# An adaLN block on one NeuronCore: early feed-forward weights, sums in DRAM, block modulation, two-bank ScalarE reads and a new warm-up tile

## The chip, the cores and the metric

One of the eight cores of a Trainium2 chip runs the whole program. The metric is the device time of one execution in microseconds; lower is better. Five engines have their own instruction streams: TensorE (PE, with its weight loads PEld), VectorE (DVE), ScalarE (ACT), GpSimd (POOL) and SyncE (SP), whose queue issues nearly all DMAs.

## The reference

The input x has 2048 tokens of 512 features, in fp32. Six modulation rows come from one product of a 512-vector with a 512 x 3072 matrix.

```python
mod = (silu(c) @ w_mod).reshape(c.shape[0], 6, 1, -1)
sa, ca, ga, sb, cb, gb = (mod[:, i] for i in range(6))
h = layernorm(x) * (1 + ca) + sa
x = x + ga * A(h)          # 32 heads of 16, 4 segments of 512 tokens
h = layernorm(x) * (1 + cb) + sb
x = x + gb * (relu(h @ w1 + b1) ** 2 @ w2 + b2)     # 512 -> 1792 -> 512
```

A projects h to q, k and v. In each segment it does causal softmax attention, reads a memory matrix M (16 x 16 a head) with phi(q) = where(q > 0, q + 1, exp(q)), mixes the two by a gate per head, and after the segment adds phi(k)^T v to M. The result goes through wo.

## The kernel before

Every fp32 operand of a large product is split into a rounded high part and the rest; a product is then three matmuls (high x high, high x low, low x high).

**Start.** Four token tiles of segment 0 and the 512 x 512 blocks of w_mod for sa and ca are loaded (`load_x`, `mod_cols`). TensorE runs warm-up products on `msk`, a tile that POOL clears (L438, L439, L546). `mod_parts` multiplies silu(c) with whole rows (L568), ScalarE copies the result (L572), and four small products a vector turn it into columns `modc` (L588, L590). Tiles are normalized (L607), turned (L616), scaled and shifted (L628, L630) and split into `HT` (L636, L638). The first q and k products (`qk` of unit 0, L747 to L749) follow.

**Attention.** There are 16 units (4 segments x 4 groups of eight heads). For each, `qk` projects (L757), ScalarE and VectorE split (L794, L796), and twelve DMAs spread the parts over the rows of `ST`, a ring of 12 slots (L812). `vproj` makes v once a segment (L837), and eight ScalarE copies put it into `VT` (L829). `a_quad` computes scores for the row maxima (L870), VectorE reduces them (L875), except the tile `ac` that ScalarE copies (L908) for POOL and VectorE; the maxima are turned (L940), negated (L942) and sent into `ST`. `b_quad` computes scores again with the maximum taken off; a pair of products fills two PSUM banks, and ScalarE takes exp of each bank (L1057); POOL masks (L1044); the products with v follow (L1099). `mem` reads and updates M (L967, L991, L993, L1001).

**Output projection and feed-forward.** `wo_tile` turns the attention result (L1241), splits it (L1248, L1250), multiplies (L1214 to L1216) and adds x (L1257). The last segment's four tiles come at the end, because they need unit 15 (L1161 to L1170). `ln2` makes seven combinations of the normalized tokens. The first layer is one step of a Strassen scheme over 2 x 2 blocks: seven products (`prod`, L1443 to L1445) in place of eight, for each of seven column pairs q and four segments. `load_w1` loads a pair (L1390), splits three blocks (L1396 on ScalarE, L1399 on VectorE), forms four sums in place (L1404, four VectorE operations) and splits these. It does so for each of the 28 pairs. `ffn1` adds up the products and squares; `ffn2` multiplies with W2 (L1502 to L1504).

**Order.** Every step is a node made by `op`, with an engine, a planned duration and the nodes it waits for. `ORDER` holds, for each engine, the node numbers in the order in which they are emitted; an engine runs them in that order. `Plan.take` gives a product its PSUM bank, the first free one. The tiles of the feed-forward stage lie in a pool that is opened when every node of the attention stage has been emitted (`open_ffn`, N_FFN).

Of the kernel before, what the change touches and what calls it, by code (L numbers as in the profile page):

```python
# [8 lines left out]
F32 = mybir.dt.float32  # L9
F32R = mybir.dt.float32r  # L10
# [8 lines left out]
P = 128  # L19
# [15 lines left out]
N_WARM = 70  # L35
# [28 lines left out]
395 520 320 280 405 324-325 434 439 392 326 407 437 446 328 449 397 330 413 442 539 768 528 769 454 770 549 771 533
547 773-774 558 775-776 552 530 421 458-460 423 415 525 462 469 873 472 429 465 935 535 936 644 477 937 657 938 431
481 561 482-483 652 563 940 570 941 573 682 942 544 943 801-802 654 566 803-804 578 649 806-807 554 808 485 809 663
487 582-583 586 668 589 584 685 671 593 659 601 596 673 1345-1346 1355-1356 676 605-607 687 835 1006 1068 694 1069 678
1070 702 848 609 1071 611 854 1073 690 1074 845 1075 697 843 1076 876 706 840 710 707-708 717 818 867 819-820 850 821
725 720 864 823-824 713 859 825 862 826 968 729 976 882 730-731 889 981 1201 869 1202 973 987 1203 978 1204 897 995
1206 1139 892 1207 885 1208 983 1209 1101 1109 879 901-902 905 733 912 903 735 915 908 992 920 1009 1000 997 924-925  # L70
1015 1106 926 1012 1018 1114 1022 1025 1002 928 1111 1142 930 1030 1034 1145 1120 1133 1038 1035-1036 1128 1045 1041
1272 1048 1363 1053 1364 1116 1365 1125 1234 1366 1242 1057-1059 1130 1148 1368 1155 1369 1151 1370 1135 1371 1163
1061 1253 1063 1167 1247 1396-1397 1239 1398-1399 1158 1266 1401-1402 1171 1403 1244 1404 1258 1168-1169 1178 1530
1181 1261 1531 1174 1532-1533 1263 1275 1186 1535-1536 1249 1537 1430 1438 1538 1468 1190-1192 1281 1413 1288 1414
1284 1415 1194 1416 1296 1196 1291 1418-1419 1268 1420 1449 1459 1443 1421 1278 1940-1941 1950-1951 1457 1435
1300-1302 1440 1304 1601 1311 1663 1314 1664 1454 1307 1665 1445 1666 1563 1471 1462 1668-1669 1319 1670 1464 1576
1671 1571 1474 1323 1582 1324-1325 1573 1796 1477 1797 1484 1798 1568 1492 1799 1487 1592 1801 1578 1802 1604 1590
1480 1803 1327 1804 1696 1329 1496 1595 1500 1497-1498 1607 1587 1507 1503 1734 1706 1510 1515 1519 1709 1610 1613
1520-1521 1617 1704 1597 1523 1620 1525 1737 1701 1625 1629 1740 1715 1633 1723 1630-1631 1640 1636 1958 1711 1959
1829 1842 1960 1834 1961 1867 1643 1963-1964 1648 1837 1965 1870 1966 1720 1652-1654 1873 1839 1743 1656 2114 1750  # L80
# [1479 lines left out]
```

## Time and profile before

| | |
|---|---|
| Median of 3 runs | 774.13 us (774.03 to 775.08) |
| Profiled execution, whole | 778.38 us |
| Its span, first to last instruction | 776.7 us |
| Mean granted TensorE clock | 0.993 |
| Busy in the span | PE 756.3, DVE 643.3, ACT 509.2, POOL 233.6 us |

The profile is of one execution. A matmul's row gives its start and a modelled end; neighbouring matmuls overlap, so the time from one start to the next is what a product costs. A row of the timeline has start, length, engine, line, operation, out<-in, shape and count, and in brackets the idle time before it with what ended it. "PE ... <- ACT ..." in the view of waits says that TensorE waited for ScalarE. PEclk is the share of the full TensorE clock that was granted in a stretch.

### The profile page before, as it was taken

How to read it: one execution, taken by the hardware profiler on the slowest of the kernel's cores; microseconds unless marked ns; L12 is line 12 of the kernel's file. 1: busy time of each engine (PE TensorE's matmuls, PEld its weight loads, DVE VectorE, ACT ScalarE, POOL GpSimd, SP SyncE). 2: the span in 40 equal slices, each digit the busy share in tenths (PEclk: the TensorE clock that was granted, in tenths of full speed). 3: DMA queues.
4: the chain of work that ended last, by engine and by line, in shares of the span. 5: the costliest groups of instructions: out<-in, count | busy, mean ns of one | idle time of the engine just before them, and what ended most of it. 6: DMA issues, size and time to landing. Idle time of an engine off the chain costs nothing.

```text
span 776.7 us, 17899 instructions
## 1 busy us (share of the span) xinstructions
PE 756.3 (97%) x6576; PEld 594.2 (77%) x6579; DVE 643.3 (83%) x1643; ACT 509.2 (66%) x990; POOL 233.6 (30%) x351
## 2 busy tenths in 40 slices
PE   8998999999999999999999989999999999999998
PEld 4777657675787858875676668888888888998896
DVE  3577877897888897789889889999989998998753
ACT  0658768879779896778756836667555665655541
POOL 3555453537665786534513310000000010000000
PEclk9999999999999999999999999999999999999999
DMA  7574661330443324244654166322351121043201
GB/s 270 174 182 107 203 182 52 89 98 23 118 124 83 98 71 103 55 116 127 167 176 132 49 201 192 96 82 82 108 174 58 41 96 55 28 136 101 63 1 54
DMA packets 78097, 84.81 MB, mean 109 GB/s; under 512 B 9014, under 2 KB 47674, under 8 KB 78011
## 3 DMA queue, kind: packets, MB, share of 16 engines
q1 hardware_dynamic: 77858, 83.55, 37.4%
q8 instruction: 52, 0.85, 0.5%
q14 instruction: 35, 0.28, 0.1%
q10 hardware_dynamic: 152, 0.13, 0.1%
HBM read 46.16 MB, written 10.49 MB: 73 GB/s over the span
## 4 chain that ended last, share of the span: by engine, by line
PE 69%; DVE 16%; ACT 6%; issue 3%; SPq 3%; DMA 2%; POOL 1%; ACTq 0%; DVEq 0%; POOLq 0%
PE bqk L757 9%; PE bpv L1099 6%; PE bpf L1502 5%; PE bpf L1504 5%; PE bpf L1503 5%; PE ba L870 5%; PE bpb L1040 5%; PE bv L837 4%; PE bhy L1443 3%; PE bhy L1444 2%; PE bhy L1445 2%; ACT pt L1057 2%; SPq L812 2%; PE bwarm L546 2%; DVE w1r L1404 2%
## 5 line engine op out<-in xcount | busy, mean ns | idle before, releaser
L875 DVE CUSTOM_DVE_ANT_0 ba<-ba,msk 128x128 f32<-128x128 f32 (+2 forms) x384 | 186.0, 542 | 33.9 <-PE ba L870 27.1
L1057 ACT ACTIVATE pt<-bpb 128x512 f32<-128x512 f32 x320 | 173.3, 616 | 31.2 <-PE bpb L1040 27.6
L1044 POOL TENSOR_SCALAR_AFFINE_SELECT pt<-pt 128x512 f32<-128x512 f32 x128 | 80.6, 649 | 93.4 <-ACT pt L1057 63.3
L1396 ACT CAST w1d<-w1r 128x768 fp32r<-128x768 f32 (+1 forms) x56 | 52.7, 944 | 76.5 <-PE bhy L1445 58.2
L757 PE MATMUL bqk<-HT,WQK 64*128 64x512 f32 x720 | 101.6, 396 | 0.0
L1502 PE MATMUL bpf<-W,rr 128*128 128x512 f32 x224 | 88.7, 396 | 0.0
L1504 PE MATMUL bpf<-W,rr 128*128 128x512 f32 x224 | 88.0, 393 | 0.0
L1503 PE MATMUL bpf<-W,rr 128*128 128x512 f32 x224 | 87.7, 391 | 0.0
L1099 PE MATMUL bpv<-pt,VT 128*32 128x512 f32 (+3 forms) x1024 | 81.3, 442 | 0.9 <-DVE mx L875 0.4
L1040 PE MATMUL bpb<-ST 64*128 64x256 f32 (+2 forms) x512 | 79.4, 350 | 2.3 <-ACT phi L803 0.4
L870 PE MATMUL ba<-ST 63*128 63x256 f32 (+2 forms) x512 | 75.1, 346 | 1.0 <-issue 0.4
L757 PEld LDWEIGHTS bqk<-HT,WQK 64*128 64x128 f32 x720 | 69.7, 186 | 8.2 <-issue 0.6
L1040 PEld LDWEIGHTS bpb<-ST 64*128 64x128 f32 x512 | 50.0, 185 | 21.2 <-ACT pt L1057 3.9
L870 PEld LDWEIGHTS ba<-ST 63*128 63x128 f32 x512 | 48.8, 187 | 19.4 <-issue 4.2
L1399 DVE TENSOR_TENSOR w1d<-w1r,w1d 128x768 fp32r<-128x768 f32 (+1 forms) x56 | 60.6, 1085 | 3.2 <-ACT w1d L1396 2.8
L1099 PEld LDWEIGHTS bpv<-pt,VT 128*32 128x32 f32 x1024 | 27.7, 110 | 38.1 <-issue 29.5
L837 PE MATMUL bv<-WVO,HT 64*128 64x512 f32 x384 | 54.9, 405 | 0.0
L875 DVE DVE_READ_ACCUMULATOR2_ANT mx<- 128x1 f32 x384 | 54.1, 141 | 0.0
L603 POOL TENSOR_SCALAR st_all<-st_all 128x4 f32<-128x4 f32 x4 | 1.8, 451 | 169.8 <-DVE st_all L596 169.8
L1404 DVE TENSOR_TENSOR w1r<-w1r 128x256 f32<-128x256 f32 x112 | 47.5, 424 | 3.2
L1481 ACT ACTIVATE r<-r,b1c 128x512 f32<-128x512 f32 x56 | 38.4, 719 | 17.8 <-DVE r L1463 17.5
L1504 PEld LDWEIGHTS bpf<-W,rr 128*128 128x128 f32 x224 | 42.0, 188 | 10.0 <-DVE rr L1489 0.3
(200 smaller groups left out, 1829.6 us busy)
## 6 DMA issues: line engine op xcount, KB each, us to landing
ST<-sg SPq DMA_DIRECT2D x192, 128.0 KB
w1r<-in_B_w SPq DMA_DIRECT2D x56, 256.0 KB
wm<-in_w_mod SPq DMA_DIRECT2D x24, 256.0 KB
xt<-in_A_x SPq DMA_DIRECT2D x16, 256.0 KB
xw<-in_A_x SPq DMA_DIRECT2D x16, 256.0 KB
wr<-in_B_w SPq DMA_DIRECT2D x14, 256.0 KB
o_dram<-on SPq DMA_DIRECT2D x12, 256.0 KB
ot<-o_dram SPq DMA_DIRECT2D x12, 256.0 KB
```

The costliest lines, as they stand in the source:

```text
L757: m = nc.tensor.matmul(bank(("qk", u, w)), W3(w, k, x, cc * P, (cc + 1) * P)[z], HT[z, y, k], start=(ph == 0 and k == 0 and i == 0), stop= ...
L837: m = nc.tensor.matmul(bank(("v", s, t)), HT[z, x, k, t * P:(t + 1) * P], WVO[z, k, y], start=(ph == 0 and k == 0 and i == 0), stop=(ph == ...
L870: nc.tensor.matmul(dst[:, c0:c0 + n], ST[b:b + 63, 0, sl, qt * P:(qt + 1) * P], ST[b:b + 63, 1, sl, :n], start=True, stop=True)
L875: nc.vector.tensor_tensor_reduce(i, i, msk[:, 512 - n:], scale=1.0, scalar=-3e38, op0=ALU.add, op1=ALU.max, accum_out=o)
L1040: nc.tensor.matmul(dst, ST[b:b + 64, 1, sl, kb * P:(kb + 1) * P], ST[b:b + 64, 0, sl, q0:512], start=True, stop=True)
L1044: nc.gpsimd.affine_select(out=ap, in_=ap, pattern=[[0, ap.shape[1]], [1, P]], compare_op=ALU.is_ge, fill=0.0, base=0, channel_multiplier=-1)
L1057: ns = [act(512, lambda j=j: nc.scalar.activation(buf("PPP"[n], pt)[:, i + j], bank(keys[j]), AF.Exp, scale=0.25), pr[slot] + 0.01 + 0.001 ...
L1099: nc.tensor.matmul(bank(o)[32 * hq:32 * hq + 32, q0:q0 + src.shape[1]], v[:, a:a + 32], src, start=start, stop=stop, tile_position=(0, 32 ...
L1404: nc.vector.tensor_tensor(r[:, o], r[:, a], r[:, b], op=f)
L1502: nc.tensor.matmul(p, rh, FF["W2"][:, f, 0], start=(f == 0), stop=False)
L1503: nc.tensor.matmul(p, rh, FF["W2"][:, f, 1], start=False, stop=False)
L1504: nc.tensor.matmul(p, rl, FF["W2"][:, f, 0], start=False, stop=(f == NF - 1))
```

## The change

1. **Warm-up.** 46 products in place of 70; they read a 128 x 128 tile `wz` that VectorE clears first, read four times over.
2. **Block modulation.** sa and ca are computed in four blocks of 128 features: two loads of 512 x 128 (rows of 512 bytes) a block, eight products with the block as weights and 64 equal columns, and one VectorE addition into `modc`. The whole-row products, the two ScalarE copies and the turning products of these two vectors go. The affine step of a feature block waits for its own block only, and the first q and k products for the first half of `HT`.
3. **ScalarE over neighbouring banks.** All of PSUM is one tile `PB`. `banks` gives a pair of products two banks side by side where it can, and one ScalarE instruction then reads both: exp, `ac`, `mt`, `pk` and the copies into `VT`. Where they are not side by side, two are issued.
4. **Early feed-forward weights.** `ST`, `SG` (the split q and k) and `AC` live to the end. Raw pairs of w1 go into `SG`, their split forms and the results `rr` into slots of `ST`; pairs 0 and 1 no longer wait for N_FFN but for the last users of these places. `u` uses the `xr` tiles.
5. **Sums in DRAM.** The first segment stores each pair's four sums (one DMA of 512 KB a pair); the other three load them instead of forming them (21 loads more, 7 stores more, 84 VectorE operations fewer) and load three of the four raw blocks.
6. **Order.** All five lists are new, with other constants in the planner. Numbers are not comparable between the lists, since nodes were added and removed.

```diff
-N_WARM = 70
+N_WARM = 46
...
+    def banks(self, k):
+        free = set(self.pools["bank"])
+        near = lambda i: (i - 1 in free) + (i + 1 in free)
+        if k == 2:
+            pairs = [(i, i + 1) for i in sorted(free) if i + 1 in free]
...
+    wz = const.tile([P, P], BF, name="wz")
+    nc.vector.memset(wz, 0.0)
...
-    ST = sb.tile([P, 2, NSLOT, 512], F32R, name="ST")
+    ST = const.tile([P, 2, NSLOT, 512], F32R, name="ST")
+    SG = const.tile([P, 4, 512], F32R, name="SG")
+    AC = const.tile([P, 2, 512], F32, name="AC")
...
+    PB = ps.tile([P, 8, 512], F32, name="PB")
...
+    def both(keys, f):
+        a, b = (PL.slot[k] for k in keys)
+        if b == a + 1:
+            f(PB[:, a:b + 1], slice(0, 2))
+        else:
+            f(PB[:, a:a + 1], slice(0, 1))
+            f(PB[:, b:b + 1], slice(1, 2))
...
-        pe("F", 0.22, lambda: nc.tensor.matmul(bank(wk_), msk[:, :P], msk, start=True, stop=True), 50.0,
+        pe("F", 0.22, lambda: nc.tensor.matmul(bank(wk_).rearrange("p (a n) -> p a n", a=4), wz, wz[:, None, :].to_broadcast([P, 4, P]), start=True, stop=True), 50.0,
...
-    n_ca = mod_cols(1, CA, 1.0, PR0 + 0.1, pool="P")
-    n_sa = mod_cols(0, SA, 0.0, PR0 + 0.2, pool="P")
-    MODC = {CA: [n_ca, n_sa]}
+    NR = 64
+    def mod_block(j):
+        c = slice(j * P, (j + 1) * P)
+        ld = [sp(lambda m=m: nc.sync.dma_start(buf("P", keys_m[m])[:, :, c],
+                                               wmod[:, m * D + j * P:m * D + (j + 1) * P].rearrange("(k p) n -> p k n", p=P)),
...
+        def mm():
+            for m in (0, 1):
+                for k in range(KD):
+                    nc.tensor.matmul(bank(b_m)[:, NR * (2 * j + m):NR * (2 * j + m + 1)], TL[keys_m[m]][:, k, c],
+                                     cs[:, k:k + 1].to_broadcast([P, NR]), start=k == 0, stop=k == KD - 1)
...
+    MODC = {CA: [mod_block(j) for j in range(KD)]}
...
-                           after=[n] if k else [*ht, *(WN[w, cc] if s == 0 else []), *ends], get=() if k or i else [("#D", b)])
+                           after=[n, *(ht[2:] if k == 2 else [])] if k else [*ht[:2], *(WN[w, cc] if s == 0 else []), *ends], get=() if k or i else [("#D", b)])
...
-        cp = [act(512, lambda j=j: nc.scalar.copy(buf("ac", ac)[:, j], bank(keys[j])), pr[0] + 0.01 + 0.001 * j, after=[first],
-                  put=[keys[j]]) for j in (0, 1)]
+        cp = [act(1024, lambda: both(keys, lambda p, w: nc.scalar.copy(buf("ac", ac)[:, w], p)), pr[0] + 0.01, after=[first], put=keys)]
...
-            ns = [act(512, lambda j=j: nc.scalar.activation(buf("PPP"[n], pt)[:, i + j], bank(keys[j]), AF.Exp, scale=0.25),
-                      pr[slot] + 0.01 + 0.001 * j, after=[k], put=[keys[j]]) for j in (0, 1)]
+            ns = [act(1024, lambda: both(keys, lambda p, w: nc.scalar.activation(buf("PPP"[n], pt)[:, i + w.start:i + w.stop], p, AF.Exp, scale=0.25)),
+                      pr[slot] + 0.01, after=[k], put=keys)]
...
+        first = s == 0 and q < 2
+        ks = kr if s == 0 else ("w1s", s, q)
+        n = sp(lambda: load(s), pr - 0.2, 1 << 19 if s == 0 else 3 << 17, 2, after=SGU if first else [], get=[("w1r", kr)])
+        h = act(768, lambda: hi(kr, 1, 4, 0), pr, sbuf=True, after=[n, *([z for pp in range(4) for z in STU[4 * (NU - 3 + q) + pp]] if first else []),
+                                                                    W1N[0, 0][0][0] if first and q else None], get=[("w1d", kd)])
+        l = dve(768, lambda: lo(kr, 1, 4, 0), pr + 0.01, after=[h], put=[kr] if s else [])
+        if s == 0:
+            n = op("DVE", 1.8, sums, pr + 0.02, after=[l])
+            W1S[q] = sp(lambda: nc.sync.dma_start(s_dram[q], raw(kr).rearrange("p b k n -> p (b k n)")), pr + 0.3, 1 << 19, after=[n], put=[kr])
+        else:
+            n = sp(lambda: nc.sync.dma_start(raw(ks).rearrange("p b k n -> p (b k n)"), s_dram[q]), pr - 0.1, 1 << 19, after=[W1S[q], n], get=[("w1r", ks)])
+        h2_ = act(1024, lambda: hi(ks, 0, 4, 3), pr + 0.03, sbuf=True, after=[n, h])
+        l2_ = dve(1024, lambda: lo(ks, 0, 4, 3), pr + 0.04, after=[h2_], put=[ks])
```

More of the change, by code (lines that the diff above doesn't have):

```diff
@@ L64 @@
[L64 to L68, printed above, removed]
@@ L278, in can @@
         return all(len(self.pools[p]) >= k for p, k in need.items())
+    def banks(self, k):
[3 more added lines that the diff above has]
+            pairs = [(i, i + 1) for i in sorted(free) if i + 1 in free]
+            if pairs:
+                got = min(pairs, key=lambda p: near(p[0]) + near(p[1]))
+            else:
+                got = sorted(free)[:2]
+        else:
+            got = [min(sorted(free), key=near)] if k == 1 else sorted(free)[:k]
+        for i in got:
+            self.pools["bank"].remove(i)
+        return list(got)
     def take(self, n):
+        got = self.banks(sum(pool[0] == "#" for pool, _ in n.get))
         for pool, key in n.get:
             if pool[0] == "#":
-                self.held[key] = [(pool, self.pools[pool].pop(0)), ("bank", self.pools["bank"].pop(0))]
+                self.held[key] = [(pool, self.pools[pool].pop(0)), ("bank", got.pop(0))]
             else:
@@ L405, in block_kernel @@
     dram = ctx.enter_context(tc.tile_pool(name="dram", bufs=1, space=bass.MemoryType.DRAM))
+    s_dram = [dram.tile([P, 8 * P], F32, name=f"s_dram{q}") for q in range(NF // 2)]
     x1_dram = [dram.tile([L, D], F32, name=f"x1_dram{s}") for s in range(NS - 1)]
@@ L1267, in ln2 @@
     def ln2(s, pr, wait=()):
-        r = op("POOL", 0.5, lambda: ln_rstd(st_all[:, 4 * s:4 * s + 4], 4), pr[0] - 0.1, after=[X1N[4 * s + t] for t in range(4)] + (XWN if s else []))
+        r = op("POOL", 1.25, lambda: ln_rstd(st_all[:, 4 * s:4 * s + 4], 4), pr[0] - 0.1, after=[X1N[4 * s + t] for t in range(4)] + (XWN if s else []))
         H2N[s] = [None] * 7
@@ L1380, in wraw, with raw, load @@
         return TL[k]
+    W1S = {}
+    halves = lambda t: t.rearrange("p (a n) -> p a n", a=2)
+    late = NU - 1
+    SGU = [n for n in PL.nodes if ("sg", late) in n.put]
+    ACU = [n for n in PL.nodes if ("ac", late, 0) in n.put or ("ac", late, 1) in n.put]
     def load_w1(s, q, pr):
         kr, kd = ("w1r", s, q), ("w1d", s, q)
-        def load():
-            TL[kr] = FF["sb"].tile([P, 4, 2, P], F32, name="w1r", tag=f"w1r{PL.slot[kr]}")
+        def raw(k):
+            if k not in TL:
+                TL[k] = SG.bitcast(F32)[:, 2 * PL.slot[k]:2 * PL.slot[k] + 2].rearrange("p a (b k n) -> p (a b) k n", b=2, k=2)
+            return TL[k]
+        def load(n0=0):
@@ L1401, in sums, with lo @@
+        def lo(k, a, b, o):
+            nc.vector.tensor_tensor(TL[kd][:, 1, o:o + b - a], raw(k)[:, a:b], TL[kd][:, 0, o:o + b - a].bitcast(F32), op=ALU.subtract)
         def sums():
[L1402 removed]
+            r = raw(kr)
             for o, a, b, f in ((1, 0, 1, ALU.add), (0, 2, 0, ALU.subtract), (2, 1, 2, ALU.subtract), (3, 3, 2, ALU.subtract)):
                 nc.vector.tensor_tensor(r[:, o], r[:, a], r[:, b], op=f)
[L1405 removed]
@@ L1429, in block_kernel @@
            get=[("xr", kb)], after=[X1N[4 * NS - 1]])
-    n_b2 = dve(512, lambda: nc.vector.tensor_tensor(gab, TL[kb], FF["gbb"], op=ALU.mult), z + 0.4, after=[n, n_gbb], put=[kb])
+    n_b2 = dve(512, lambda: nc.vector.tensor_tensor(halves(gab), halves(TL[kb]), FF["gbb"], op=ALU.mult), z + 0.4, after=[n, n_gbb], put=[kb])
     F1, F2 = {}, {}
+    STZ = [z for pp in range(4) for z in STU[4 * late + pp]]
     OUTN = []
```

396 lines of the change are left out of this document (196 added, 200 removed), and 18 rows, old and new, of the table ORDER.

## The prediction

> **What bounds the kernel now.** I read the page first, then the stages, then the start, the waits and the clock.
>
> ```profile
> span 776.7 us, 17899 instructions
> PE 756.3 (97%) x6576; PEld 594.2 (77%) x6579; DVE 643.3 (83%) x1643; ACT 509.2 (66%) x990; POOL 233.6 (30%) x351
> PE 69%; DVE 16%; ACT 6%; issue 3%; SPq 3%; DMA 2%; POOL 1%; ACTq 0%; DVEq 0%; POOLq 0%
> ```
>
> The second line is busy time, the third the shares of the chain that ended last. TensorE is busy 97% of the span and is 69% of the chain: what the change can win is the 20 us in which TensorE does nothing, the warm-up products, which compute nothing, and time at a lowered clock. VectorE's 16% of the chain counts only where TensorE waits.
>
> The same by stage (columns: stretch, length, then busy us of PE, PEld, DVE, ACT, POOL with counts, PEclk, DMA share, GB/s):
>
> ```profile
> 60.00:120.00 60.00, 57.45 (x650) 40.15 (x652) 47.44 (x162) 46.49 (x109) 30.15 (x39) 0.97 0.59 170
> 120.00:200.00 80.00, 78.26 (x943) 55.00 (x939) 66.87 (x232) 67.33 (x158) 44.91 (x68) 0.98 0.24 64
> 200.00:300.00 100.00, 98.46 (x1198) 76.02 (x1197) 84.71 (x289) 82.49 (x193) 69.04 (x105) 1.00 0.38 97
> 300.00:400.00 100.00, 99.04 (x1030) 70.33 (x1027) 85.80 (x286) 73.03 (x164) 41.14 (x64) 1.00 0.45 122
> 400.00:450.00 50.00, 49.41 (x410) 32.63 (x410) 45.00 (x113) 33.30 (x69) 13.98 (x23) 1.00 0.36 109
> 460.00:540.00 80.00, 78.96 (x499) 69.63 (x498) 78.05 (x135) 50.09 (x74) 0.00 (x0) 1.00 0.38 113
> 540.00:640.00 100.00, 99.54 (x630) 88.92 (x629) 94.63 (x164) 60.05 (x81) 2.15 (x2) 1.00 0.33 101
> ```
>
> TensorE is idle 2.6, 1.7, 1.5, 1.0 and 0.6 us in the five attention stretches (7.4 in 390 us) and 1.5 us in the two of the feed-forward. VectorE is 98% busy in 460 to 540, and still TensorE hardly waits there.
>
> The sum is made against the profiled execution: 776.7 of span and 1.7 around it, 778.4; that lies 4.25 above the median of 774.1, and I carry the same changes over to the median.
>
> **1. Start: warm-up tile and block modulation.**
>
> ```profile
> 1.51 0.10 PEld L546 LDWEIGHTS <-msk 128*128 128x128 bf16 x1 [1.51 <-POOL msk L438]
> 3.27 8.83 PE L546 MATMUL bwarm<-msk 128*128 128x512 bf16 x32 [3.27 <-POOL msk L439]
> 12.18 3.19 PE L546 MATMUL bwarm<-msk 128*128 128x512 bf16 x14
> 16.51 1.04 PE L616 MATMUL blnq<-ident,xt 128*128 128x128 f32 x8
> 21.08 1.84 PE L588 MATMUL bmodc<-selc,t 128*128 128x1 f32 x16
> 25.52 0.38 PE L747 MATMUL bqk<-HT,WQK 128*128 128x256 f32 x1 [0.42 <-ACT HT L636]
> 26.33 0.39 PE L748 MATMUL bqk<-HT,WQK 128*128 128x256 f32 x1 [0.43 <-DVE HT L638]
> 10.02 1.92 DVE L607 TENSOR_SCALAR xt<-xt,mv 128x512 f32<-128x512 f32 x4 [1.49 <-POOL mv L604]
> 23.16 1.15 ACT L628 ACTIVATE xt<-blnq,modc 128x256 f32<-128x256 f32 x2 [0.47 <-DVE modc L590]
> 24.33 1.14 ACT L636 CAST HT<-xt 128x512 fp32r<-128x512 f32 x2
> 24.98 1.29 DVE L638 TENSOR_TENSOR HT<-xt,HT 128x512 fp32r<-128x512 f32 x2 [0.23 <-ACT HT L636]
> 0.00:10.00 10.00, 6.73 (x24) 2.80 (x25) 5.38 (x13) 1.59 (x2) 6.88 (x25) 1.00 0.81 273
> ```
>
> Before, the first weights of `msk` load at 1.51 and the first product starts at 3.27, when POOL's second clearing is done. One small tile needs one clearing, so the start can be near 1.5. The warm row is 8.83 for 32; the later one is 3.19 for 14, 0.22 each, and 8.83 comes out with nine at 0.43 and 23 at 0.22, so the clock rose near 7.0. From 1.5 to 7.0 there is room for 13 slow ones. In the new order 32 warm-ups precede the first modulation product (55 before), so the other 19 end at 7.0 + 4.1 = 11.1. A block has 16 small products of the shape of the 1.84 row: 0.115 each, 1.84 a block, as the weights are of that size and the 64 columns are few. Two blocks to 14.8; the 16 transposes at 1.04 / 8 = 0.13, 2.0, to 16.8; block 2 to 18.7, block 3 to 20.7, five warm-ups to 21.8. There the first q product starts, which before took 26.33 for its second member to run. Seven warm-ups against four lie among the first products (+0.65). 26.33 − 21.8 − 0.65 = **3.9**.
>
> Are the data there? Eight loads of 256 KB and four token tiles, with what lies between them, are 3.25 MB: at 273 GB/s 11.9 us, from 2.7 to 14.6; a load in rows of 512 bytes may go slower, and block 3's comes last and is wanted at 18.7. The norms end at 11.9 (10.02 row). The first half of `HT` needs two affine steps (1.15), the cast (0.57) and the rest (0.65): 2.4 after block 1, 17.2, and so in time. Bounds: −7 when the clock rises a window earlier too, −1 when the last block's loads are 3 us late.
>
> **2. ScalarE over two banks.**
>
> ```profile
> 443.03 1.09 ACT L1057 ACTIVATE pt<-bpb 128x512 f32<-128x512 f32 x2
> L1057 ACT ACTIVATE pt<-bpb 128x512 f32<-128x512 f32 x320 | 173.3, 616 | 31.2 <-PE bpb L1040 27.6 <-PE ba L870 1.7 <-POOL pt L1044 0.8
> L1487 ACT ACTIVATE r<-r 128x1024 f32<-128x1024 f32 x28 | 29.7, 1061 | 0.8
> PEld bpb L1040 <- ACT pt L1057: 3.9, 13, 0.4
> PEld ba L870 <- ACT pt L1057: 2.8, 7, 0.9
> PEld ba L870 <- ACT ac L908: 2.5, 4, 0.8
> PEld bpb L1040 <- ACT mt L942: 1.2, 3, 0.8
> PEld bpv L1099 <- issue: 29.5, 118, 0.8
> ```
>
> From the diff, 268 ScalarE instructions go: 160 exp, 32 `ac`, 32 `mt`, 12 `pk`, 32 `VT`. Two single exps back to back end 1.09 after the first starts, so they overlap already; one instruction of 1024 elements takes about 1.04 (1061 ns in SBUF). That is 0.05 a pair, 13 us of the 302.6 that ScalarE is busy in the five stretches. What reaches the end is what TensorE waited for: the four rows (total us, count, longest) make 10.4 us in 27 waits. A lead of two pairs, 0.1 us, at each of 27 is 2.7; I take **−2.5**, since TensorE's own idle time there is 7.4 for all releasers together. Bounds 0 and −10.4.
>
> The Trainium skill, "ScalarE: Activation LUTs", section "What ACT_TABLE_LOAD costs", gives an ACTIVATE as 186 ns + 0.833 ns an element, with about 93 ns of overlap for neighbours. By it a merged pair would save 93 ns, 25 us of ScalarE in all, and this term would be −4.7, an estimate; the single length agrees (612 against 616), the pair does not (1131 against 1090).
>
> **3. New order.** The last row above is TensorE waiting with nothing but its own queue, 29.5 / 118 = 0.25 each, where products of one shape class follow another. Counted in the two lists, the changes between row-tiled, column-tiled and full products fall from 154 to 146. Eight at 0.25 are 2.0; half lies beside a product still running: **−1.0**. The lists are otherwise all new, and a wait can appear at any place; half of the 7.4 us idle either way, so ±3.
>
> **4. Clock.**
>
> ```profile
> 60.00:70.00 10.00, 9.00 (x76) 8.77 (x78) 7.08 (x18) 7.96 (x24) 3.21 (x5) 0.83 0.44 110
> 180.00:190.00 10.00, 9.78 (x112) 4.84 (x104) 7.28 (x25) 8.61 (x20) 6.84 (x9) 0.83 0.15 40
> 450.00:460.00 10.00, 7.10 (x34) 5.43 (x33) 7.99 (x19) 2.81 (x4) 3.01 (x4) 0.83 0.80 232
> 60.61 0.27 PE L991 MATMUL bpkt<-ident,phi 64*128 64x64 f32 x1 [1.28 <-DVE sg L796]
> 453.40 0.78 PE L1241 MATMUL bwot<-ident,X1L 128*128 128x128 f32 x5 [2.60 <-DVE X1L L1170]
> ```
>
> Three stretches of 10 us have a granted clock of 0.83: 3.4 us at half speed, which costs 1.7 us each. One follows the wait of 1.28, one that of 2.60; the third, at 180, follows no long wait but a stretch of small products. With other waits the windows lie otherwise. I take one gone, the one after the 2.60 (step 5 fills part of it): **−1.7**; bounds −5.1 and +1.7 (one more).
>
> The Trainium skill, "TensorE: Matmul & The Clock Gate", section "Why this matters for your kernels", says that throughput drops in mid-kernel are avoided when no idle gap exceeds about 3 us. By it none of the three should be there and the term would be 0, 765.0 in all; the trace contradicts it, with 1.28 and 2.60.
>
> **5. Early feed-forward weights.**
>
> ```profile
> 460.46 0.37 PE L1443 MATMUL bhx<-H2a,w1d 128*128 128x256 f32 x1
> L1399 DVE TENSOR_TENSOR w1d<-w1r,w1d 128x768 fp32r<-128x768 f32 x28 | 26.6, 952 | 2.9 <-ACT w1d L1396 2.6 <-ACT u L1456 0.3
> 450.55 0.99 SPq L1390 DMA_DIRECT2D w1r<-in_B_w  x2
> ```
>
> Before, the pair's loads are issued at 450.55 and the first feed-forward product starts at 460.46. In the new order a first-layer product of six members (0.12 each) stands before the last output tiles, in the 2.60 us wait: −0.7. Against it, the rest of pair 0 on VectorE (0.95) moves into 400 to 450, where VectorE is 90% busy; the next output tile's norms come later by half of it, +0.5. **−0.2**, bounds −2.6 and +1. The loads now wait for the last users of `ST` and `SG` three units from the end; behind them on SP's queue stand the feed-forward weights, needed 10 us later.
>
> **6. Sums in DRAM.**
>
> ```profile
> L1404 DVE TENSOR_TENSOR w1r<-w1r 128x256 f32<-128x256 f32 x112 | 47.5, 424 | 3.2
> PEld bhy L1443 <- DVE r L1463: 3.1, 8, 0.8
> ```
>
> 84 of the 112 sums go, 84 × 0.424 = 35.6 us of VectorE. TensorE waited for VectorE in this stage 3.1 us in eight waits: with VectorE at 98% half of them go, **−1.5** (0 to −3.1). SP issues 28 DMAs more, 0.5 us each (the 450.55 row: two in 0.99), 14 us over 320. The seven stores wait on SP for VectorE's sums, and with them what is queued behind: pieces of W2 and raw blocks. The cover is the first-layer products of the pair in hand, 14 products and four output tiles, over 10 us; without it each store would hold back the next pair by VectorE's four sums, 1.7 us. The loads' traffic, 21 × 0.5 MB over 300 us, is 37 GB/s on a stretch that moves 101 to 113. Taken at 0.
>
> **Sum.** −3.9 − 2.5 − 1.0 − 1.7 − 0.2 − 1.5 = −10.8: 778.4 becomes 767.6, the median **763.3**.
>
> **The rivals.**
>
> *B, only the start comes through.* TensorE's waits for ScalarE move to VectorE (84.71 and 85.80 of 100 busy) and the clock windows stay three: −3.9 and −1.0 of the sums: **769.2**. For it: TensorE idle is 7.4 us, spread among many releasers.
>
> *C, ScalarE stops being waited for.* A merged exp saves up to 2 × 0.616 − 1.061 = 0.17 where a pair was not back to back; 268 × 0.17 = 46 us of 302.6. Then all 10.4 of the waits go, and with them two of the clock windows, 3.4: −3.9 − 10.4 − 1.0 − 3.4 − 0.2 − 1.5 = −20.4, **753.7**. Against it: 31.2 us of idle time before 320 exps says that most follow directly. The skill's rule named in step 2 lies between this and the forecast.
>
> *D, slower: banks come free later.* A merged exp gives both banks back at its end, so the first one 1.04 − 0.62 = 0.42 us later than now. If every one of the 27 waits is for a pair's first bank, and gets longer by that, they grow by 27 × 0.42 = 11.3 in place of −2.5. −8.3 + 11.3 = +3.0, **777.1**. It decides from 0.31 us a wait. For it: 82.49 of 100 busy in 200 to 300. Against it: eight banks, and the order is written for the merged length.
>
> *E, the change does not do what it says.* Banks are seldom neighbours, so two instructions are issued as before, and the blocks' loads come late: **774.1**.
>
> **How the numbers follow.** Forecast 0.58, B 0.18, C 0.11, D 0.07, E 0.06. The forecast's own range is 758 to 768 (start −7, or order +3 and no clock window gone). 752 to 772 takes in B and C and leaves out D and E. About 0.2%, 1.5 us, is the least that a measurement of this kernel can tell from no change. Faster by more: forecast, B, C: 0.87. Within: 0.06. Slower: 0.07.
>
> **What would show it.** Step 1: the first warm-up before 2 us and the first q product near 22. Step 2: about 160 exps of 1.0 to 1.1 us; waits of weight loads for exp under 5 us; if they are above 10, D. Step 3: fewer waits on issue than 118. Step 4: two stretches with a clock under 0.9, none at 450. Step 5: a first-layer product before the last output tiles. Step 6: VectorE's busy share in 460 to 540 near 85%, and 28 sums. The prediction is wrong if the new lists bring a long wait of their own, above all at the blocks' loads or where the stores stand in SP's queue.

## The result and the profile after

In the first comparison the changed kernel took 769.61 us (median of 4 runs, 767.92 to 770.89) against 774.54 before: a ratio of 0.9935, interval 0.9914 to 0.9956, faster by 4.9 us. A second one, with 6 and 18 runs, gave 0.9921 (0.9897 to 0.9944). Over all runs the medians are 776.08 (the 93 runs of before whose clock is on record, 773.8 to 780.5) and 769.73 (10 runs): **6.3 us faster**, where 10.8 was forecast. The three runs shown ahead of the prediction lay at the low end of that spread. The versions below ran beside before on five chips, on which before's medians were 776.0 to 777.4; the ratios given are to the runs on the same chip.

The page of the changed kernel, first lines and chain:

```profile
span 768.1 us, 17662 instructions
PE 749.4 (98%) x6587; PEld 594.6 (77%) x6587; DVE 614.0 (80%) x1564; ACT 497.6 (65%) x790; POOL 233.7 (30%) x351
PE 85%; ACT 4%; DVE 3%; SPq 2%; DMA 2%; issue 2%; POOL 1%; DVEq 0%; ACTq 0%; POOLq 0%
```

VectorE works 29 us less and its share of the chain falls from 16% to 3%. ScalarE issues 200 instructions fewer, not 268. Its stages (columns as before):

```profile
60.00:120.00 60.00, 57.33 (x658) 38.59 (x654) 46.86 (x168) 45.95 (x78) 33.11 (x44) 1.00 0.61 173
120.00:200.00 80.00, 76.75 (x968) 54.26 (x968) 68.47 (x237) 65.40 (x114) 48.17 (x76) 1.00 0.31 78
300.00:400.00 100.00, 98.42 (x977) 70.77 (x977) 86.95 (x281) 69.18 (x109) 38.62 (x63) 1.00 0.48 132
460.00:540.00 80.00, 80.00 (x511) 72.02 (x510) 77.58 (x131) 52.77 (x76) 0.00 (x0) 1.00 0.51 160
540.00:640.00 100.00, 99.93 (x641) 89.97 (x640) 80.39 (x125) 61.09 (x85) 1.61 (x2) 1.00 0.41 130
```

In the feed-forward TensorE has no idle time left (it had 1.04 and 0.46). In the attention it is idle longer than before: 3.25 against 1.74 in 120 to 200, 1.58 against 0.96 in 300 to 400. Idle time is no measure of the attention's length, though, as a_oldsplit shows below. VectorE is still 97% busy in 460 to 540 (77.58 of 80), where the prediction looked for near 85%; segment 0 forms its sums there as before.

The start, in the timeline of TensorE:

```profile
1.04 5.73 PE L567 MATMUL PB<-wz 128*128 128x512 bf16 x13 [1.04 <-DVE wz L427]
6.89 4.29 PE L567 MATMUL PB<-wz 128*128 128x512 bf16 x19
11.01 3.68 PE L706 MATMUL PB<-cs,wm 128*128 128x64 f32 x32
21.96 0.36 PE L799 MATMUL PB<-HT,WQK 128*128 128x256 f32 x1 [0.54 <-DVE modc L714]
```

Thirteen slow products, the first block at 11.0, two blocks in 3.7, the first q product at 22.0: the start is as forecast (11.1, 3.7, 21.8). The warm-up products go from 0.43 to 0.22 us apart, that is, the clock rises, at 6.9 us here.

To see each stage I split every trace at three TensorE products, by their start times: the last of the first 48 q and k products (start), the last transpose of the attention's results (attention), the end of the first quarter of the first-layer products (transition and segment 0), the last of them (the rest). A half-clock window is a stretch, 3.41 us or two or three times that long, in which TensorE's granted clock is 0.5; half of its length is taken off in the last three columns. That correction is exact only where a window meets no wait; attention values without a window in them are marked *.

| kernel | median (runs) | start | attention | to first quarter | rest |
|---|---|---|---|---|---|
| before, profile | 776.08 (93) | 32.2 | 414.5 | 84.5 | 224.2 |
| before_again | | 33.3 | 413.6 | 84.6 | 224.2 |
| after | 769.73 (10) | 28.8 | 415.8* | 79.7 | 223.5 |
| after_again | | 28.7 | 416.2* | 81.0 | 223.4 |
| a_split | 768.52 (5) | 27.7 | 414.4* | 79.8 | 223.4 |
| a_splitexp | 769.16 (6) | 28.3 | 414.6* | 80.0 | 223.7 |
| a_sums | 779.53 (7) | 28.8 | 415.7* | 80.9 | 232.6 |
| b_nosums | 773.41 (11) | 32.6 | 412.9 | 84.4 | 222.1 |
| b_wz | 774.76 (12) | 30.1 | 412.8 | 84.2 | 224.2 |
| a_warm | 768.06 (6) | 26.6 | 414.0 | 81.0 | 223.4 |
| a_late | 775.87 (12) | 28.4 | 416.6* | 83.6 | 223.5 |
| a_late2 | 771.93 (8) | 28.7 | 416.3* | 81.4 | 223.5 |
| a_fifo | 769.29 (6) | 28.4 | 414.3 | 80.8 | 223.5 |
| a_old | 766.10 (10) | 28.5 | 411.9 | 80.6 | 223.5 |
| a_old_again | | 28.5 | 412.9* | 80.8 | 223.5 |
| a_oldsplit | 767.61 (6) | 28.4 | 414.2 | 80.8 | 223.5 |
| a_warmfifo | 766.40 (6) | 26.2 | 413.8 | 81.5 | 223.5 |
| a_oldwarm | 767.09 (6) | 26.1 | 412.5 | 79.9 | 223.5 |

Four things have to be known to read this table.

- In the attention the correction takes off too much. The same attention is 411.9 with a window and 412.9 without (a_old, a_old_again), and 414.0 with two (a_warm) where five traces without one have 415.7 to 416.6. A window there cost about 0.7 us and not 1.7. With 0.7, the four traces of before's attention are 413.8 to 416.5.
- The start is not corrected for when the clock rose: 6.9 us in before, 9.1 in before_again, 7.0 and 6.5 in the two traces of the changed kernel, 5.0 in b_wz, by the clock record of each trace. A us later costs about half a us of the start (before_again's is 1.1 longer than before's).
- The new order moves six products with W2 (0.23 each, 1.4 us) from the third column to the fourth: 126 and 492 of them before, 120 and 498 after. On the same work the third column gains 2.1 to 3.5 and the fourth 2.1.
- The time behind the last first-layer product is in no column: 16.2 us before and 17.0 after, in both traces of each.

So the gain is 3.4 to 4.6 in the start, 2.1 to 3.5 in the transition and segment 0, and 2.1 in the rest; the end gives 0.8 back and the attention about 1 (1.3 to 2.6 by the table as it stands): about 7 in all. The mean clock over all runs is 0.9944 before and 0.9961 after, 0.0017 x 775 = 1.3 us more at most. The medians say 6.3 for everything, so a stage read from single profiles is good to 1 or 2 us.

### The profile page after: what moved, and what is told of

It is laid out like the page before. It is cut to its first block, busy times and chain, and to the rows that moved or that the text cites. A ratio compares the mean times of both kernels' runs of the same rounds, so it can differ in the third digit from the quotient of the medians.

```text
span 768.1 us, 17662 instructions
## 1 busy us (share of the span) xinstructions
PE 749.4 (98%) x6587; PEld 594.6 (77%) x6587; DVE 614.0 (80%) x1564; ACT 497.6 (65%) x790; POOL 233.7 (30%) x351
## 4 chain that ended last, share of the span: by engine, by line
PE 85%; ACT 4%; DVE 3%; SPq 2%; DMA 2%; issue 2%; POOL 1%; DVEq 0%; ACTq 0%; POOLq 0%
PE PB L809 9%; PE PB L1149 8%; PE PB L1573 7%; PE PB L1574 7%; PE PB L1572 7%; PE PB L1511 6%; PE PB L1512 6%; PE PB L1513 6%; PE PB L1090 5%; PE PB L922 5%; PE PB L890 4%; ACT pt L1107 2%; PE PB L1264 2%; SPq L864 2%; PE PB L1266 2%; PE PB L1265 2%
## 5 line engine op out<-in xcount | busy, mean ns | idle before, releaser
L927 DVE CUSTOM_DVE_ANT_0 PB<-PB,msk 128x128 f32<-128x128 f32 (+2 forms) x384 | 186.3, 543 | 31.1 <-PE PB L922 23.6
L1107 ACT ACTIVATE pt<-PB 128x1024 f32<-128x1024 f32 (+1 forms) x191 | 162.4, 898 | 34.1 <-PE PB L1090 30.1
L809 PE MATMUL PB<-HT,WQK 64*128 64x512 f32 x720 | 103.9, 397 | 0.0
L1572 PE MATMUL PB<-W,ST 128*128 128x512 f32 x224 | 88.7, 396 | 0.0
L1573 PE MATMUL PB<-W,ST 128*128 128x512 f32 x224 | 88.5, 395 | 0.0
L1574 PE MATMUL PB<-W,ST 128*128 128x512 f32 x224 | 88.5, 395 | 0.0
L1149 PE MATMUL PB<-pt,VT 128*32 128x512 f32 (+3 forms) x1024 | 80.5, 437 | 0.8 <-DVE mx L927 0.6
L1090 PE MATMUL PB<-ST 64*128 64x256 f32 (+2 forms) x512 | 77.5, 353 | 2.8 <-ACT pt L1107 2.6
L809 PEld LDWEIGHTS PB<-HT,WQK 64*128 64x128 f32 x720 | 72.0, 185 | 8.2 <-ACT SG L846 0.4
L922 PE MATMUL PB<-ST 63*128 63x256 f32 (+2 forms) x512 | 73.8, 343 | 2.8 <-ACT pt L1107 1.7
L1459 DVE TENSOR_TENSOR ST<-SG,ST 128x768 fp32r<-128x768 f32 (+1 forms) x56 | 60.5, 1085 | 7.8 <-ACT ST L1456 7.8
L1550 ACT ACTIVATE AC<-AC,b1c 128x512 f32<-128x512 f32 x56 | 38.3, 718 | 28.3 <-DVE AC L1532 28.3
L1511 PE MATMUL PB<-H2a,ST 128*128 128x256 f32 x196 | 55.6, 284 | 0.0
L1512 PE MATMUL PB<-H2a,ST 128*128 128x256 f32 x196 | 55.2, 281 | 0.0
L1513 PE MATMUL PB<-H2a,ST 128*128 128x256 f32 x196 | 55.1, 281 | 0.0
L1149 PEld LDWEIGHTS PB<-pt,VT 128*32 128x32 f32 x1024 | 28.2, 109 | 32.6 <-issue 24.3
```

Source lines behind the costliest of these rows:

```text
L809: m = nc.tensor.matmul(bank(("qk", u, w)), W3(w, k, x, cc * P, (cc + 1) * P)[z], HT[z, y, k], start=(ph == 0 and k == 0 and i == 0), stop= ...
L922: nc.tensor.matmul(dst[:, c0:c0 + n], ST[b:b + 63, 0, sl, qt * P:(qt + 1) * P], ST[b:b + 63, 1, sl, :n], start=True, stop=True)
L927: nc.vector.tensor_tensor_reduce(i, i, msk[:, 512 - n:], scale=1.0, scalar=-3e38, op0=ALU.add, op1=ALU.max, accum_out=o)
L1090: nc.tensor.matmul(dst, ST[b:b + 64, 1, sl, kb * P:(kb + 1) * P], ST[b:b + 64, 0, sl, q0:512], start=True, stop=True)
L1107: ns = [act(1024, lambda: both(keys, lambda p, w: nc.scalar.activation(buf("PPP"[n], pt)[:, i + w.start:i + w.stop], p, AF.Exp, scale=0.25 ...
L1149: nc.tensor.matmul(bank(o)[32 * hq:32 * hq + 32, q0:q0 + src.shape[1]], v[:, a:a + 32], src, start=start, stop=stop, tile_position=(0, 32 ...
```

## Experiments

The theories after the result: (1) a merged read gives a pair's first bank back late, so the merge costs; (2) the choice of neighbouring banks costs, not the merge; (3) the gain behind the attention is VectorE's relief, or (4) the early weights.

**before_again and after_again: the clock of many runs.** No edit.

> The kernel before, unchanged, for the granted clock of each of its runs. Theory 'the profile was not typical': most runs have a mean clock of 0.997 or more (one half-clock window of 3.4 us or none), and the 4.25 us by which the profiled execution lay above the median are two windows, 3.4 us. Rival 'profiling costs it': every run shows about 0.993 as the profiled execution did, and the 4.25 come from elsewhere. Time 774 to 775 either way.

> The changed kernel, unchanged, as the base of the next kernels: 769.6 (768 to 771). Its clocks were 0.993 to 0.997 in four runs; if before's are higher, the term of the clock in the prediction had the wrong sign for the median.

Measured: 775.76 (774.06 to 777.31, 12 runs, clocks 0.993 to 0.998) and 769.80 (766.61 to 771.07, 6 runs, 0.993 to 0.999). Both expectations of before_again fall between: most runs stand at 0.995, two windows and a bit. Among the 93 runs, the 18 with 0.997 or more have a median of 774.3, the 45 near 0.995 775.9, the 21 at 0.992 or less 778.1. The number of windows changes from run to run; the profiled 778.4 was a run with three. The three runs ahead of the prediction have no clock on record; their times are those of runs with fewer windows.

**a_split, a_splitexp: the merge undone.**

```diff
-        if b == a + 1:
+        if False:
```

That is a_split. a_splitexp makes the same change for exp alone; the other reads stay merged.

> The changed kernel with two ScalarE instructions everywhere, one a bank; places, banks and order as they are. Theory 'banks come free later' (the waits of TensorE for exp, 8.3 + 5.5 + 2.6 + 1.7 in place of 3.9 + 2.8, are waits for the first bank of a merged read): faster by 2 to 4 us, 766 to 768, and these rows fall to about those of before. Theory of the prediction (less ScalarE work helps): slower by about 2.5, 772. Rival 'the order': the waits come with the new lists, and it stays within 1 us of 769.6.

> The changed kernel with two instructions for exp alone; ac, mt, pk and VT stay merged. Theory 'the first bank of an exp pair comes late': all of a_split's gain or more, 768.5 or 768. If the gain came from the other merges it stays at 769.7. TensorE's rows of waits for exp tell it beside the time: about 8 and 6 with the merge.

Measured: 768.52 (ratio to before 0.9909, 0.9890 to 0.9928) and 769.16 (0.9904, 0.9885 to 0.9923), against 769.73. The intervals overlap with the changed kernel's, so the times alone do not decide; the attention, 414.4 and 414.6 against 415.7 to 416.6 in the five traces with merged reads, none of them with a window, does: as the change was made, merging cost 1 to 2 us there. The forecast gain, by which a_split would have been near 772, is refuted for this kernel. The waits that theory 1 names were these, in the changed kernel, 60 to 450:

```profile
PEld PB L1090 <- ACT pt L1107: 8.3, 16, 0.8
PEld PB L922 <- ACT pt L1107: 5.5, 13, 0.8
PE PB L1090 <- ACT pt L1107: 2.6, 7, 0.6
PE PB L922 <- ACT pt L1107: 1.7, 4, 0.5
PEld PB L922 <- ACT AC L960: 2.1, 3, 0.8
```

The two of exp on weight loads are twice as long as before (3.9 and 2.8); together they are 13.8, above the 10 that the prediction named as the sign of rival D. But in a_split they are 7.8 and 5.8, with single reads. They do not come from the merge; only the two PE rows (2.6 and 1.7) do, which a_split does not have. The length of a merged exp was as forecast (1.04), but 31 of the 160 pairs did not find neighbouring banks:

```profile
L1107 ACT ACTIVATE pt<-PB 128x1024 f32<-128x1024 f32 x129 | 130.1, 1031 | 30.4 <-PE PB L1090 26.4 <-DVE mx L927 1.0 <-PE PB L922 0.5
L1107 ACT ACTIVATE pt<-PB 128x512 f32<-128x512 f32 x62 | 34.0, 620 | 3.8 <-PE PB L1090 3.7
```

**a_fifo: single reads (`if False`, as in a_split), and the banks as before.** The old kernel took the bank that had been free longest. The change takes the pair (or single bank) with the fewest free neighbours, in order of number, which may be one just freed.

```diff
     def banks(self, k):
-        free = set(self.pools["bank"])
...
+        return [self.pools["bank"].pop(0) for _ in range(k)]
```

> The changed kernel with two ScalarE instructions everywhere, as a_split, and PSUM banks given as before: the one that has been free longest. TensorE waits for exp 13.6 us on its weight loads in a_split and 6.7 before, though both use single instructions. Theory 'the choice of banks': a bank side by side is often one just freed, so the waits fall to about 7, attention from 414.4 to about 412, 766.5. Rival 'the new order makes the waits': no change from a_split, 768.5.

Measured: 769.29 (766.38 to 770.84), not faster than a_split. The waits for exp did fall, to 5.2 and 2.4, and the time did not follow. Theory 2 in its simple form is refuted: with single reads the choice of banks changes these waits, and not the time by more than the scatter.

**a_old, a_old_again: merged reads, oldest banks.** Of the pairs side by side, the one whose younger bank has been free longest; single banks oldest first.

```diff
     def banks(self, k):
-        free = set(self.pools["bank"])
...
+        free = self.pools["bank"]
+        pairs = [(i, i + 1) for i in free if i + 1 in free] if k == 2 else []
+        got = min(pairs, key=lambda p: max(free.index(i) for i in p)) if pairs else free[:k]
...
```

> The changed kernel with merged reads, but among the pairs side by side the one free longest is taken, and single banks longest free first; fewer pairs are side by side. Theory 'the choice of banks': faster than 769.7 by 1 to 2. Rival 'merged reads free the banks late': no gain while most pairs are merged, 769 to 770.

> a_old once more, on the same chip as a_late2: 765.5 (764.7 to 767), 0.9855 of before. If it was a lucky place of the half-clock windows, the clock falls to 0.995 and the time rises to 767 to 768.

Measured: 765.50 (764.72 to 766.72; ratio 0.9855, 0.9833 to 0.9878) and 766.45 (763.50 to 767.10; 0.9867, 0.9844 to 0.9890). Together 766.10, 3.6 below the changed kernel, and the attention is 412.9 against 416.0, neither with a half-clock window in it. Almost as many exps are merged as in the changed kernel:

```profile
L1099 ACT ACTIVATE pt<-PB 128x1024 f32<-128x1024 f32 x126 | 127.2, 1031 | 31.1 <-PE PB L1082 27.4 <-POOL phi L850 1.0 <-DVE mx L919 1.0
```

So it is the same merge with other banks. The waits that shrank most are those for VectorE's row maxima (`mx`); the views do not say whether for the bank that it reads or for the maxima. Those for exp fell less (8.3 and 5.5 to 7.7 and 4.4). First the changed kernel, then a_old, 60 to 450:

```profile
PEld PB L1090 <- DVE mx L927: 2.7, 7, 0.4
PEld PB L922 <- DVE mx L927: 2.3, 7, 0.5
PEld PB L991 <- DVE mx L927: 1.9, 3, 0.9
PEld PB L1184 <- DVE mx L927: 1.2, 3, 0.8
```

```profile
PEld PB L1082 <- DVE mx L919: 1.6, 4, 0.4
PEld PB L914 <- DVE mx L919: 1.1, 4, 0.4
PEld PB L983 <- DVE mx L919: 0.8, 1, 0.8
```

8.1 us against 3.5. These rows hold waits of the weight loads, part of which lies beside a running product, so the 4.6 is a bound and not the gain.

**a_oldsplit: the merge alone, with good banks.** a_old with `if False` as in a_split.

> a_old with two ScalarE instructions everywhere: same order, same banks, nothing merged. Theory 'merged reads help where the banks have been free long': slower than a_old by 1 to 3, 767 to 769. Theory 'merged reads give the first bank back late and cost whatever the banks': faster than a_old, 764.5 or less. Theory 'the banks alone': within 1 us of 765.5.

Measured: 767.61 (766.75 to 769.12; ratio 0.9892, 0.9869 to 0.9914). With the oldest banks, merging is worth 1.5 us by the medians, and 2 to 3 by the ratios; with the change's banks it cost about 1. The sign of the merge hangs on which banks are taken. Why single reads gain so little from better banks (768.52 to 767.61) while merged ones gain 3.6 the rows of waits do not tell: a_oldsplit's waits for `mx` are as low as a_old's. The score products tell more. First a_old, then a_oldsplit:

```profile
L1082 PE MATMUL PB<-ST 64*128 64x256 f32 (+2 forms) x512 | 75.8, 352 | 3.0 <-ACT pt L1099 2.9
L914 PE MATMUL PB<-ST 63*128 63x256 f32 (+2 forms) x512 | 71.5, 343 | 3.3 <-ACT pt L1099 1.7
```

```profile
L1082 PE MATMUL PB<-ST 64*128 64x256 f32 (+2 forms) x512 | 82.2, 354 | 1.0 <-ACT xt L644 0.2
L914 PE MATMUL PB<-ST 63*128 63x256 f32 (+2 forms) x512 | 76.8, 345 | 0.9 <-ACT pt L1099 0.2
```

They are issued in pairs, one product on each half of TensorE's rows, each with its own bank. One product takes as long in both kernels (352 and 354 ns in the first row), but with single reads the time in which some of them runs is 159.0 us in place of 147.3, though TensorE is idle less (5.2 us between 30 and 440, against 9.5). In the median the two of a pair start 3 to 5 ns apart, but in some pairs the second starts later, and the two halves then work in part one after the other. Summed over the 512 pairs, the second starts 11.4 and 12.9 us late in a_old and a_old_again and 30.4 in a_oldsplit; it is 16.5 and 15.8 in the changed kernel, 30.9 in a_split and 22.9 in before. So the pairs stay together better with merged reads, which give both banks back at once. That is something merging can buy, against the later release of the first bank; the prediction had counted ScalarE's time alone. How much of the 1.5 to 3 us it makes was not tested apart.

**b_nosums, a_sums: VectorE's 35.6 us.** In before the later sums are left out; in after they are put back beside the loads.

```diff
             r = TL[kr]
+            if s:
+                nc.vector.tensor_tensor(r[:, 1, 0:1, 0:1], r[:, 0, 0:1, 0:1], r[:, 1, 0:1, 0:1], op=ALU.add)
+                return
```

```diff
-        l = dve(768, lambda: lo(kr, 1, 4, 0), pr + 0.01, after=[h], put=[kr] if s else [])
+        l = dve(768, lambda: (lo(kr, 1, 4, 0), sums() if s else None), pr + 0.01, after=[h], put=[kr] if s else [])
```

> The kernel before; in segments 1 to 3 the four sums of each pair are left out (one VectorE operation on one element stands for them, so the sums used there are wrong): VectorE gets 35.6 us less, all else stays. From the profiles, the last three quarters of the first-layer products take 224.0 us before and 223.3 after, and the excess of TensorE's steps behind 540 us is 6.4 before and 5.2 after: theory 'the sums are worth about 1 us in the old order': faster by 0.5 to 1.5, 774.5. Prediction's step 6: faster by 1.5 (0 to 3.1). Rival from a_sums (9.7 us for the same work in the new order): faster by 5 or more.

> The changed kernel, which still loads the sums, with the four VectorE operations of each of the 21 later pairs put back (their results are not used): only VectorE's 35.6 us return. Prediction: slower by 1.5, 771.1. Theory 'the relief is the larger part of the gain behind 450 us' (4.7 us less there in the profiles): slower by 3 to 5, 773 to 774. Rival 'VectorE is covered': no change.

Measured: b_nosums 773.41 (0.9964, 0.9949 to 0.9980), 2.7 faster, of which the rest of the feed-forward gives 2.1 (224.2 to 222.1). a_sums 779.53, 9.7 slower than the changed kernel, of which 9.1 in the rest. The stretch 540 to 640 of a_sums:

```profile
540.00:640.00 100.00, 97.33 (x617) 85.93 (x618) 91.57 (x158) 56.90 (x78) 1.61 (x2) 1.00 0.39 122
```

VectorE is busy 91.6 there, less than before's 94.6, and yet TensorE is idle 2.7 us, where it was 0.5. VectorE's work is the same; the order, it seems, is not made for it. That a_sums does the four sums in one block behind the split, and keeps the loads, was not tested apart. So 35.6 us of VectorE are worth 2.1 in the old order, and 9 to an order that counts on their absence. From before to after, the rest gains 2.1 on the same work, as b_nosums does.

**a_late, a_late2: the early weights undone.** Pairs 0 and 1 wait for N_FFN, and their nodes are moved behind the attention in the lists; in a_late2 VectorE's and ScalarE's also behind the two output tiles' splits.

```diff
-        n = sp(lambda: load(s), pr - 0.2, 1 << 19 if s == 0 else 3 << 17, 2, after=SGU if first else [], get=[("w1r", kr)])
+        n = sp(lambda: load(s), pr - 0.2, 1 << 19 if s == 0 else 3 << 17, 2, after=[*SGU, N_FFN] if first else [], get=[("w1r", kr)])
```

> The changed kernel with the early weights undone: pairs 0 and 1 wait for N_FFN again, pair 0's work on ScalarE and VectorE stands behind the attention, and the first feed-forward product behind the last output tiles' first products. The time from the last attention product to the end of the first quarter of first-layer products, half-clock time taken off, is 84.5 before and 79.7 to 81.0 after. Theory 'early weights made this gain': back to about 84, 773 in all. Prediction's step 5 (0.2): 770. Rival 'the new order of the rest of segment 0 made it': within 1 us of 769.7.

> a_late with a milder undo: pair 0's and 1's work on ScalarE and VectorE stands behind the splits of the two output tiles (in a_late VectorE waited for pair 0's load ahead of such a split, and TensorE 6.01 us for it). Theory 'early weights made the gain of the transition': first-layer products to the first quarter end near 83 to 84 after the last attention product, 772 to 774. Rival 'a_late's loss was its own placement and clock': 770 to 771, and the time stays near 81.

Measured: 775.87 and 771.93 (0.9948, 0.9928 to 0.9968). a_late misled: its own placement made VectorE wait for the load ahead of an output tile, and the clock fell for three windows.

```profile
454.77 0.79 PE L1275 MATMUL PB<-WVO,ST 128*128 128x512 f32 x1 [6.01 <-DVE ST L1309]
450.00:460.00 10.00, 5.23 (x12) 4.12 (x13) 8.16 (x14) 3.68 (x5) 0.00 (x0) 0.50 0.83 255
```

a_late2 has no such wait; the old one is back, and the stage is 81.4, 0.4 to 1.7 above the changed kernel's:

```profile
447.96 1.33 PE L1303 MATMUL PB<-ident,X1L 128*128 128x128 f32 x5 [2.24 <-DVE X1L L1232]
```

The early weights are worth 2.2 us by the medians, of which 0.4 to 1.7 show in this stage and the rest in the clock (mean 0.9946 against 0.9961). The other 1.7 us of this stage come with the new order of segment 0: the change's lists move VectorE's normalizing of the feed-forward tokens, sums and splits, and TensorE's waits of 0.15 to 0.36 us for VectorE that before has at 468, 486, 499, 510 and 538 us, 1.04 in all, are gone. That was not tested apart.

**b_wz, a_warm: the start.**

```diff
+    wz = sb.tile([P, P], BF, name="wz")
+    nc.vector.memset(wz, 0.0)
...
-        pe("F", 0.22, lambda: nc.tensor.matmul(bank(wk_), msk[:, :P], msk, start=True, stop=True), 50.0,
+        pe("F", 0.22, lambda: nc.tensor.matmul(bank(wk_).rearrange("p (a n) -> p a n", a=4), wz, wz[:, None, :].to_broadcast([P, 4, P]), start=True, stop=True), 50.0,
```

```diff
-        pe("F", 0.22, lambda: nc.tensor.matmul(bank(wk_).rearrange("p (a n) -> p a n", a=4), wz, wz[:, None, :].to_broadcast([P, 4, P]), start=True, stop=True), 50.0,
+        pe("F", 0.22, lambda i=i: None if 20 <= i < 32 else nc.tensor.matmul(bank(wk_).rearrange("p (a n) -> p a n", a=4), wz, wz[:, None, :].to_broadcast([P, 4, P]), start=True, stop=True), 50.0,
```

> The kernel before with the new warm-up tile alone, all 70 products. They can start at 1.0 in place of 3.3. Theory 'the start is a fixed list of products': 2.2 us more at the slow clock, five products at 0.43, each of which would have cost 0.22 later: faster by about 1.1, 774.7. Rival 'loads bound the start': no change. Rival 'the clock rises a window earlier': faster by 2 or more.

> The changed kernel with 12 of the 32 warm-up products ahead of the first modulation block left out (12 x 0.22 = 2.6 us). Theory 'the start is a fixed list of products, not bound by loads': faster by 1.5 to 2.6, 767 to 768, and the first q product near 19.5. Rival 'loads': blocks come every 1.5 us at 340 GB/s, the last near 11.5, and the q product stays near 22. Rival 'clock': an idle gap lowers it, slower.

Measured: b_wz 774.76 (0.9983, 0.9968 to 0.9998), 1.3 faster, and its start ends 2.0 to 3.1 earlier. With the clock rising as long after the first warm-up product as in before (3.6 us) that would be 2.2, where the changed kernel would have 4.5: the warm-up tile is about half of the start's gain, the blocks the other half. a_warm 768.06 (0.9890, 0.9869 to 0.9910), 1.7 below the changed kernel, first q product at 20.4. All 12 products were expected to lie ahead of the first block; in the trace 24 stand there in place of 32, so 8 went there (1.8 us) and 4 behind it, and a wait for a block's load gives back a part:

```profile
9.42 3.76 PE L706 MATMUL PB<-cs,wm 128*128 128x64 f32 x32 [0.40 <-DMA wm<-in_w_mod]
```

So the loads begin to limit the start when 24 warm-ups precede the blocks, and 32 were too many.

**a_warmfifo, a_oldwarm: gains joined.**

> a_fifo and the 12 warm-up products left out: the two gains are in different stages and should add up. a_warm is 1.7 below the changed kernel, a_split 1.2, and the choice of banks 0 to 2: 764.8 to 766.8.

> a_old (merged reads, banks free longest) without the 12 warm-up products: the two gains lie in different stages. The gain of 1.7 of a_warm off 765.5: 763.8 (763 to 765). If the start's order shifts the attention's waits, it stays near 765.

a_warmfifo is a_fifo, and a_oldwarm is a_old, without the 12 warm-up products. Measured: 766.40 (0.9870, 0.9849 to 0.9892) and 767.09 (764.24 to 769.92; 0.9889, 0.9862 to 0.9917). The first adds up, as far as its parts are known. The second does not: its profile has the shortest span of all (762.5), but its runs show a mean clock of 0.9927 where a_old's show 0.9966. That is up to 3.0 us (0.0039 x 767), enough to take the gain. **a_old has the lowest time: 766.1, 0.9855 to 0.9867 of before;** a_warmfifo is level with it within the scatter.

## Why the prediction was wrong

The sign was right and the amount was not: 10.8 forecast, 6.3 measured over all runs (4.9 in the first comparison).

- *Start, −3.9.* Right: 28.7 against 32.2 and 33.3, by the working given; 3.4 between the two profiles in which the clock rose at nearly the same time (6.9 and 7.0).
- *ScalarE, −2.5.* This step failed. Its length was right (1.03), its cover was not. Merging cost about 1 us, and with other banks it gains 1.5 to 3. The prediction read the waits of before and shortened them; it left out that the change also chooses the banks differently, so that the waits are others, and that 31 of the 160 exp pairs would not be side by side. It also counted ScalarE's lead alone, and not that the two products of a pair start together more often where their banks come free together. It had priced a late bank only as rival D, as a property of the merged read.
- *Order, −1.0.* The attention as a whole was forecast at −3.5 with the ScalarE term, and became about 1 us longer; a_split, with single reads, is 414.4, within before's 413.8 to 416.5. The fewer mode changes cannot be seen in the sum, though the queue's own waits did fall:

```profile
PEld PB L1149 <- issue: 24.3, 110, 0.4
```

- *Clock, −1.7.* Near in size (at most 1.3 over the means), but by luck, for the place was wrong: the window behind the attention stayed, and lasted twice as long in the profile:

```profile
440.00:450.00 10.00, 7.26 (x66) 4.55 (x58) 9.49 (x26) 3.18 (x5) 3.43 (x6) 0.86 0.54 172
450.00:460.00 10.00, 10.00 (x50) 8.62 (x51) 8.67 (x15) 2.98 (x5) 0.00 (x0) 0.80 0.86 263
447.47 1.33 PE L1291 MATMUL PB<-ident,X1L 128*128 128x128 f32 x5 [1.01 <-DVE X1L L1220]
449.78 0.80 PE L1264 MATMUL PB<-WVO,ST 128*128 128x512 f32 x1 [0.99 <-DVE ST L1298]
```

  The 2.60 us wait fell to 1.01, another of 0.99 follows, and the clock fell all the same, at 447.3, within the first of them.
- *Early weights −0.2, sums −1.5.* Together −1.7 forecast, −4.2 to −5.6 measured. The sums were sized well: the rest of the feed-forward, where they went, gained 2.1 on the same work, and b_nosums 2.1. The early weights were not: 2.2 by the undo, a part of it through the clock, and the transition and segment 0, with the new order in them, gained 2.1 to 3.5. SP's new waits cost nothing that shows, as forecast. The 0.8 that the end of the kernel gives back had no term.
- *The base.* The changes were carried to a median of three runs that were faster than most. Against it the forecast time was 763.3; against the 776.1 of many runs the same sum gives 765.3. The remaining gap of 4.4 is the attention (about 4.5 in place of the forecast gain) and the end (0.8), less the larger gain of the feed-forward (2.5 to 3.9); 1 to 3 us of it lie in no stage that these readings resolve.

Rival B named the right time (769.2), partly by luck: one of its conditions, that the ScalarE term does not come through, held; its others, three clock windows and almost nothing from the feed-forward, did not. C and E did not happen. D's sign for the merge held with the change's banks; its size did not (about 1 us, not 11.3 more of waits), and a later release is not the whole cause, since merged reads gain with other banks.

## What to carry to other kernels

When a change merges reads by putting operands side by side, the allocation is part of the change: cost the choice of buffers separately from the instruction, try the ones that have been free longest, and ask which products start together when buffers come free together. What freed engine time is worth depends on the order written around it: the same 35.6 us were worth 2.1 in one list and 9 in another. Judge a kernel near full use by many runs with their clocks, not by three; before comparing stages, count that the same products lie in them; and take each undo experiment's own new waits off before reading it.

## What the runs showed of the hardware

- A ScalarE instruction over two neighbouring PSUM banks of 512 fp32 elements took 1031 ns, against 620 for one bank in the same run: the bank border costs nothing that shows. The Trainium skill, "ScalarE: Activation LUTs", section "What ACT_TABLE_LOAD costs", would have 1039 for that length, an estimate by its formula, which agrees; it says nothing of the border.
- TensorE's granted clock fell to 0.5 for 3.41, 6.83 or 10.24 us at a time, and where and how often it does so differs between runs of the same kernel (0.989 to 0.998 in 93 runs, 774 to 780 us). In all 18 traces each such window began a whole number of 3.413 us after the clock had first risen (16, 52 and 131 of them in before, 129 in the changed kernel). The longest wait alone does not decide: in the changed kernel the clock fell within a wait of 1.01, in a_old behind one of 1.75, and in a_warmfifo, with waits of 1.73 and 0.58 in the same place, it did not fall. The Trainium skill, "TensorE: Matmul & The Clock Gate", section "Why this matters for your kernels", warns of idle gaps over about 3 us; in the changed kernel the clock fell though no gap in the 15 us before was longer than 1.01.
- Two score products on the two halves of TensorE's rows ran at the same time where their banks came free together (starts 3 to 5 ns apart, about 350 ns each).
